# A state-space scan and its feed-forward block on one core: how the first two pairs of chunks load C and their products of a

## The chip, the cores and the metric

The kernel runs on one core of a Trainium2 chip. A core has five engines that run side by side: TensorE (PE: matrix products, its weight loads shown as PEld), VectorE (DVE), ScalarE (ACT), GpSimd (POOL) and SyncE (SP), which here does nothing but issue DMA transfers. ScalarE can issue transfers too. All transfers are moved by the same 16 DMA engines. The metric is the device time of one execution in microseconds; three runs of the kernel before took 359.32, 360.47 and 360.80 us, median 360.47.

## The reference

Two blocks, one after the other. First a selective state-space scan over 4 batches, 8 heads, 768 tokens, head dimension 32 and state size 16, in chunks; then a feed-forward block with a parametric ReLU on the 3072 tokens of 256 features that come out.

```python
# per batch and head; a in (0, 1], cum = running sum of log(a) in a chunk
L = np.exp(cum[..., :, None] - cum[..., None, :]) * causal      # decay from j to i
y_intra = einsum('ij,jd->id', (C @ B.T) * L, x)
y_inter = (C @ state) * exp(cum)
state = exp(sum(la)) * state + sum_j B_j x_j * exp(cum_end - cum_j)
# then, over all tokens
h = y @ w_in                                   # 256 x 2048
g = maximum(h, 0) + alpha * minimum(h, 0)
out = g @ w_out                                # 2048 x 256
```

All inputs are float32 but w_in and w_out, which arrive as float64 and have to be turned into float32 on the core.

## The kernel before

**Tiles.** The 3072 tokens are 24 chunks of 128 tokens. Two chunks make a pair (12 pairs), two pairs a group of 512 tokens (6 groups). The feed-forward block works on groups: hidden features 128 at a time (w_in, PReLU), then products with w_out. Group 0 uses plain products (`hidden`, `hidden_two`, `output`); groups 1 to 5 use a scheme of seven block products in the place of eight (`quad`, `product`), between which the scan stages of the next pairs are placed (`ssm`).

**Decays.** No logarithm is taken: the decay from j to i is a running product of a. Multiply-add scans on VectorE make it, with a (its first element of each chunk zero) as the factor and an identity as the addend. Pairs 0 and 1 are done by `first_two`, in quarter chunks of 64 tokens (`HQ`). There, TensorE spreads a from "(head, state) on partitions" to 64 partitions (`spread`, L852), VectorE scans the result (`scan`, L858), the gram of B and C is made by TensorE (`gram_of`, L868) and multiplied into it (`times`, L874). `added` (L882) makes the new states' increments, `states` (L897) chains them, `mask` (L903, GpSimd) spreads them by heads, `x_products` (L916) and `state_products` (L928) give y, which `copy_out` (L936) writes as xT, the input of the feed-forward block.

From pair 2 on the running products come from DRAM: `rows_products` (L438) scans all rows of a, writes them (`pf`, L441), and `load_products` (L167) reads them back, spread over partitions, as `ap` of a pair. Pair 2's state (L631) and its decays (L556, from `abc`, another spread copy) follow on VectorE.

**Layouts of B and C in pairs 0 and 1.** B is loaded with one token on each partition (`nat[:, 0, k]`, L203; 64-byte pieces) and turned by TensorE (`turned_b`, L842). C is loaded by `load_blocks` (L191) in 512-byte pieces, four blocks of 32 partitions, and turned by a 32 x 32 transpose on VectorE (`turned_c`, L828). C times a parity mask gives `cz` (L836, ScalarE). For pair 0, C is loaded by ScalarE's queue, all else by SP.

**Pair 0's and 1's running products** (`pf0`, `pf1`) come from a scan over their own a (`running`, L958), after `first_a` (L530 and L433) has made the scan's input.

**Weights.** Each of 16 pieces of 512 KB (`load_next`, L254) is made float32 by ScalarE (L270, L280 or L283), VectorE or GpSimd (L275), VectorE (sign bits, L293; L305), and at last GpSimd (L327). The pieces alternate between w_in and w_out from the second on.

**Fillers.** `keep_warm` (L335) issues products of constants whose result nobody reads.

**Order.** The schedule is written out by hand: each engine runs its instructions, and SP issues its transfers, in the order of the code. A transfer that waits holds back all that SP issues after it. SP's order at the start is: a, B, x of pair 0; a of pair 1; two w_in pieces; z (rows of a); C, B, x of pair 1; a w_in and a w_out piece; B, C, x of pair 2; five weight pieces; pf; abc; a weight piece; ap.

Of the kernel before, what the change touches and what calls it, by code (L numbers as in the profile page):

```python
# [22 lines left out]
def kernel(  # L23
# [47 lines left out]
    WARM = 512  # L71
# [97 lines left out]
    def load_pair(gp, decays=True):  # L169


        b, c = divmod(2 * gp, CPB)
        turned = gp > GC
        nat = ldx.tile([P, 3, 2, H * N], F32, name="nat")
        xt = ldx.tile([P, 2, HD], F32, name="xt")

        ap = ldx.tile([P, 2 * Q], F32, name="ap")
        if gp == 0:
            load_a(ap, b, c)
        elif gp > NB:  # L180
            load_products(gp, ap)
        if gp == 0:
            load_rows(0, nc.scalar)
        abc = []
        later = []

        def load_blocks(o, src, e, eng=nc.sync):


            first = src[b, e : e + 1, c * Q : (c + 2) * Q, :]  # L190
            eng.dma_start(out=o, in_=bass.AP(tensor=first.tensor, offset=first.offset,  # L191
                                             ap=[[2 * S * N, P // 32], [8 * N, 32], [1, 8 * N]]))

        for e in range(2 if gp < NB else 0):
            load_blocks(nat[:, 1, e], C, e, nc.sync if gp else nc.scalar)
        if gp == 0:
            nc.scalar.dma_start(out=al_n, in_=moe_alpha.rearrange("(k p) -> k p", p=P))
        if gp >= HALF:
            load_tokens(nat[:, 0], B[b], c * Q)
        for k in range(2 if gp < HALF else 0):  # L200
            ts = slice((c + k) * Q, (c + k + 1) * Q)
            for i, src in enumerate((B,) if turned or gp < NB else (B, C)):
                nc.sync.dma_start(out=nat[:, i, k].rearrange("p (h n) -> p h n", h=H),  # L203
                                  in_=src[b, :, ts, :].rearrange("h p n -> p h n"))

            def load_x(k=k, ts=ts):
                nc.sync.dma_start(out=xt[:, k].rearrange("p (h d) -> p h d", h=H),
                                  in_=x[b, :, ts, :].rearrange("h p d -> p h d"))

            if gp < NB:  # L210
                later.append(load_x)
            else:
                load_x()
        for load_x in later:
            load_x()
        if gp == 0:
            loads["a", 1] = prep.tile([P, 2 * Q], F32, name="a1")
            load_a(loads["a", 1], b, c + 2)
        for i, src in enumerate((B, C) if turned else ()):

            for e in range(2):
                load_blocks(nat[:, 1 + e, i], src, e)
        for k in range(2 if gp >= NB else 0):
            abc.append(lda.tile([P, H * Q], F32, name="abc"))
        loads["p", gp] = nat, abc, xt, ap
        if gp >= HALF:
            load_tokens(xt, x[b], c * Q)
        if decays:
            load_spread(gp, b, c)

# [106 lines left out]

    keep_warm(ps_h.tile([P, GT], F32, name="hp"), 1, WARM)
    keep_warm(ps_h.tile([P, GT], F32, name="hp"), 1)
# [4 lines left out]
    for v in range(2):  # L344
        vs = slice(HQ * v, HQ * (v + 1))
        nc.vector.tensor_copy(out=ident_q[vs].rearrange("p (c t) -> p c t", c=4),
                              in_=ident[vs, vs].unsqueeze(1).to_broadcast([HQ, 4, HQ]))
    bmask = const.tile([P, HD], F32, name="bmask")
# [17 lines left out]

    lent = [gp.tile([P, 4, Q], F32, name="gt", tag="gt") for i in range(4)]
# [3 lines left out]
    starts = [t.rearrange("p k t -> p (k t)") for t in (lent[0][:, :2], lent[3][:, 2:])]  # L371
    nc.gpsimd.memset(starts[0], 0.0)
# [109 lines left out]
    def rows_short(r):  # L482


        nc.vector.memset(r[:, ::HQ], 0.0)
        pr = lent[3][:RW, 1]
        nc.vector.tensor_tensor_scan(out=pr[:, ::-1], data0=r[:, 1:][:, ::-1],
                                     data1=ends_q[:RW, ::-1], initial=0.0, op0=ALU.mult,
                                     op1=ALU.add)
        return pr  # L490
# [319 lines left out]
    def first_two():  # L810
# [15 lines left out]
        def turned_c(nat):  # L826
            bc = work.tile([P, 4, Q], F32, name="bc")
            nc.vector.transpose(  # L828
                bc[:, 2:].rearrange("p k t -> p (k t)").rearrange("p (c b) -> p b c", b=8),
                nat[:, 1].rearrange("p e (b n) -> p b e n", n=N))  # L830
            return bc
# [7 lines left out]

        def turned_b(nat, tp, bc):  # L840
            for k in range(2):
                nc.tensor.transpose(tp[:, k * P : (k + 1) * P], nat[:, 0, k], ident)  # L842
            nc.scalar.copy(out=bc[:, :2].rearrange("p k t -> p (k t)"), in_=tp[:, : 2 * Q])
# [99 lines left out]
        def ss():  # L943
            return ps_s.tile([P, 512], F32, name="ss")
# [12 lines left out]
        def running(i, z, pf):  # L957
            nc.vector.tensor_tensor_scan(out=pf, data0=z.rearrange("p k t -> p (k t)"),  # L958
                                         data1=starts[i], initial=0.0, op0=ALU.mult,
                                         op1=ALU.add)  # L960

# [5 lines left out]
        clamp(nc.gpsimd, starts[0][:, ::HQ], ap0[:, ::HQ])  # L967
# [5 lines left out]
        load_pair(1)  # L973
        nat1, _, xt1, pf1 = loads["p", 1]
        scan(0, 0, sp[0])
        bc0 = turned_c(nat0)
        for r in range(1, 4):
            scan(0, r, sp[r])
        rows_turn("short", prq)
        tp = spare()  # L980
        turned_b(nat0, tp, bc0)
# [6 lines left out]
        hp = spare()  # L988
        keep_warm(hp, 1)
        gram_of(bc0, cz0, sp)  # L990
        dps = dps_in([hp, tp])
        added(dps, bn0, xt0)
        for r in (0, 1):
            times(0, r, sp[r])
        running(0, z0, pf0)
        nc.gpsimd.memset(starts[1], 0.0)
        z1 = first_a(loads["a", 1], nc.gpsimd, lent[1][:, 2:])
        clamp(nc.gpsimd, starts[1][:, ::HQ], loads["a", 1][:, ::HQ])
        cd0 = decayed_c(bc0, pf0)
        states(0, dps, pf0)  # L1000
        one_at_a_time(0, range(3))
        for r in (2, 3):
            times(0, r, sp[r])
        load_next(2)
# [9 lines left out]
        keep_warm(sp[0], 1)  # L1014
# [9 lines left out]
        bc1 = turned_c(nat1)  # L1024
# [5 lines left out]
        running(1, z1, pf1)  # L1030
        bn1 = pair_loads(1)
        convert_next(first=False)
        cz1 = spread_c(bc1)
        own = [ss(), ss()]
        turned_b(nat1, own[0], bc1)
        dps = dps_in(own)
        added(dps, bn1, xt1)
# [3 lines left out]
        states(1, dps, pf1, range(3))  # L1041
        gram_of(bc1, cz1, sp)
        one_at_a_time(1, range(3))
        for r in range(4):
            times(1, r, sp[r])
        states(1, dps, pf1, (3,))
        prelu_of[0]()
        convert_a(*pieces[2])
        sign(*pieces[2])

        def among(i, k):
            if (i, k) == (1, 0):
# [5 lines left out]
        prelu_of[2] = hidden_two(0, 2, 0, spare(), among)  # L1058
# [363 lines left out]
    sign(*pieces[3])  # L1422
# [141 lines left out]
```

## Time and profile before

| | |
|---|---|
| runs (us) | 359.32, 360.47, 360.80; median 360.47 |
| profiled execution | 360.79 us, span of its instructions 359.1 us |
| TensorE busy | 351.4 us (98%), 2979 products |
| VectorE, ScalarE, GpSimd busy | 239.5, 171.5, 204.6 us |
| DMA | 30.06 MB, of which the SP queue 29.25 MB, in 34.9% of the 16 engines' time |
| granted TensorE clock | 0.99 of full speed over the span |

All times in the profile are microseconds from the first instruction. Lines of the page give an engine's busy time; the chain of waits follows the last instruction back through what released each step; a timeline gives each instruction's start, length, source line, operands and, in brackets, how long the engine had been idle and what ended that. "x2" after a matrix product counts machine instructions: a float32 product is two. L numbers are lines of the kernel before.

### The profile page before, as it was taken

What the parts mean: (1) busy time and instruction counts of PE and PEld (TensorE: products, weight loads), DVE (VectorE), ACT (ScalarE), POOL (GpSimd) and SP (SyncE); (2) the same over time, 40 slices, a digit from 0 to 9 for tenths busy, and PEclk for the clock granted to TensorE, in tenths of its full rate; (3) what the DMA queues carried; (4) which work ended last, traced back from release to release, by engine and by line L of the source; (5) the groups of instructions that cost most, each with busy time, mean ns of one, the idle gap of its engine ahead of it and who ended that gap; (6) DMA issues with size and microseconds to landing.
All of it is one profiled execution on the core that took longest, in us unless ns stands there. A gap on an engine that the chain in (4) does not pass through costs nothing.

```text
span 359.1 us, 7762 instructions
## 1 busy us (share of the span) xinstructions
PE 351.4 (98%) x2979; PEld 286.7 (80%) x2979; DVE 239.5 (67%) x483; ACT 171.5 (48%) x389; POOL 204.6 (57%) x229
## 2 busy tenths in 40 slices
PE   6999999999999999999999999999999999999996
PEld 3676656668888888888888888888888888888885
DVE  6798795998937856866656856657856634643363
ACT  3358746535354445445345445445445444443431
POOL 6667548579847947526546536537536545434510
PEclk9699999999999999999999999999999999999999
DMA  6899889505436502402522421521101001001102
GB/s 130 184 190 355 238 215 240 135 2 120 127 88 145 108 3 62 101 15 57 91 62 53 92 64 48 97 64 43 32 2 29 2 2 29 2 1 29 33 0 58
DMA packets 101701, 30.06 MB, mean 84 GB/s; under 512 B 75728, under 2 KB 97568, under 8 KB 101664
## 3 DMA queue, kind: packets, MB, share of 16 engines
q1 hardware_dynamic: 100984, 29.25, 34.9%
q8 instruction: 23, 0.38, 0.4%
q10 hardware_dynamic: 680, 0.32, 0.3%
q14 instruction: 14, 0.11, 0.1%
HBM read 26.19 MB, written 3.37 MB: 82 GB/s over the span
## 4 chain that ended last, share of the span: by engine, by line
PE 89%; DMA 4%; DVE 4%; ACTq 0%; issue 0%; POOL 0%; ACT 0%; DVEq 0%
PE bank L1199 33%; PE hp L1224 28%; PE bank L1125 6%; PE ss L1224 6%; PE hp L1078 3%; DMA pf<-rpf 2%; PE ss L776 1%; DVE dec L556 1%; PE ss L720 1%; DMA ap<-pf 1%; DMA nat<-in_C_dram 1%; PE bank L335 1%; PE bank L1192 1%; PE ss L794 1%; PE ss L768 1%; PE bank L868 1%
## 5 line engine op out<-in xcount | busy, mean ns | idle before, releaser
L1281 POOL TENSOR_TENSOR gt<-gt 128x512 f32<-128x512 f32 x58 | 74.2, 1279 | 21.1 <-DVE gt L1209 16.2
L1199 PE MATMUL bank<-gt,w_out 128*128 128x256 f32 x320 | 83.6, 382 | 0.0
L1199 PEld LDWEIGHTS bank<-gt,w_out 128*128 128x128 f32 x320 | 60.3, 190 | 9.1 <-issue 1.0
L1209 DVE SCALAR_TENSOR_TENSOR gt<-hp,s_mul,gt 128x256 f32<-128x256 f32 x96 | 42.0, 479 | 29.0 <-ACT gt L1207 26.8
L1271 POOL TENSOR_TENSOR gt<-gt 128x512 f32<-128x512 f32 x20 | 25.4, 1271 | 62.9 <-DVE gt L1209 57.0
L1207 ACT ACTIVATE gt<-hp,s_alpha 128x256 f32<-128x256 f32 x96 | 40.3, 471 | 34.6 <-PE hp L1224 31.4
L1199 PE MATMUL bank<-gt,ws 128*128 128x256 f32 x224 | 55.9, 379 | 0.0
L1199 PEld LDWEIGHTS bank<-gt,ws 128*128 128x128 f32 x224 | 42.4, 190 | 5.5
L1224 PE MATMUL hp<-xs,w_in 128*128 128x256 f32 x160 | 41.9, 385 | 0.0
L1224 PE MATMUL hp<-xs,ws 128*128 128x256 f32 x160 | 41.2, 380 | 0.0
L1250 DVE TENSOR_TENSOR hp<-hp,u 128x512 f32<-128x512 f32 x20 | 14.0, 700 | 35.2 <-ACT u L1248 35.2
L1224 PEld LDWEIGHTS hp<-xs,ws 128*128 128x128 f32 x160 | 30.4, 190 | 4.3 <-POOL xs L1166 0.2
L1224 PEld LDWEIGHTS hp<-xs,w_in 128*128 128x128 f32 x160 | 29.8, 190 | 4.4
L1125 PE MATMUL bank<-w_out,gt 128*128 128x256 f32 x128 | 31.2, 386 | 0.9 <-POOL w_out L327 0.9
L1125 PEld LDWEIGHTS bank<-w_out,gt 128*128 128x128 f32 x128 | 23.6, 190 | 7.9 <-issue 3.1
L1224 PE MATMUL ss<-xT,w_in 128*128 128x256 f32 x96 | 24.6, 379 | 0.0
L634 POOL TENSOR_TENSOR sm<-state,bmask 128x256 f32<-128x256 f32 (+1 forms) x10 | 6.2, 619 | 29.8 <-DVE state L631 29.8
L1078 PE MATMUL hp<-xT,w_in 128*128 128x512 f32 x48 | 22.8, 597 | 0.0
L550 DVE TENSOR_TENSOR_SCAN dec<-abc,bank 128x192 f32<-128x192 f32 x48 | 22.7, 523 | 0.0
L1239 ACT COPY m<-hp 128x512 f32<-128x512 f32 x8 | 4.7, 586 | 35.7 <-PE hp L1224 35.7
L1248 ACT COPY u<-hp 128x512 f32<-128x512 f32 x20 | 11.7, 585 | 19.4 <-PE hp L1224 19.4
L1209 DVE SCALAR_TENSOR_TENSOR gt<-c,s_mul,gt 128x256 f32<-128x256 f32 x40 | 20.6, 556 | 0.0
(231 smaller groups left out, 614.2 us busy)
## 6 DMA issues: line engine op xcount, KB each, us to landing
abc<-z SPq DMA_DIRECT2D x24, 192.0 KB
raw<-in_moe_w_in_dram SPq DMA_DIRECT2D x8, 512.0 KB
raw<-in_moe_w_out_dram SPq DMA_DIRECT2D x8, 512.0 KB
abc<-z SPq DMA_DIRECT2D x8, 512.0 KB
out_dram<-o_sb SPq DMA_DIRECT2D x32, 64.0 KB
nat<-in_B_dram SPq DMA_DIRECT2D x26, 64.0 KB
xt<-in_x_dram SPq DMA_DIRECT2D x12, 128.0 KB
xt<-in_x_dram SPq DMA_DIRECT2D x24, 64.0 KB
```

Of the source, the lines that this page charges most:

```text
L550: nc.vector.tensor_tensor_scan(out=dv[:, o : o + SQ], data0=abc[k][:, s : s + SQ], data1=ident_p[0][:, :SQ], initial=0.0, op0=ALU.mult, op ...
L634: nc.gpsimd.tensor_tensor(out=sm[:, :nk].rearrange("p k (g m) -> p k g m", g=2), in0=new[:, :nk].unsqueeze(2).to_broadcast([P, nk, 2, 2 * D]),
L1078: nc.tensor.matmul(hp, w_in[:, k, f * P : (f + 1) * P], xts[g][:, k], start=(k == 0), stop=(k == KC - 1))
L1125: nc.tensor.matmul(pos[0][t // 2][:, t % 2], gt[:, t * Q : (t + 1) * Q], w_out[:, f], start=(f == 0 and t % 2 == 0), stop=(f == NF - 1), s ...
L1199: nc.tensor.matmul(ms[g][i][:, h], w, blocks[g, z][n][:, p], start=(q == 0 and h == 0), stop=(q == NQ - 1), skip_group_check=True)
L1207: nc.scalar.mul(o[:, p], h[:, p], s_alpha[:, fs[p]])
L1209: nc.vector.scalar_tensor_tensor(out=o[:, p], in0=h[:, p], scalar=s_mul[:, fs[p]], in1=o[:, p], op0=ALU.mult, op1=ALU.max)
L1224: nc.tensor.matmul(to[:, p], w(2 * z + p), b, start=start and p == 0, stop=True, skip_group_check=True)
L1248: nc.scalar.copy(out=u2, in_=A)
L1250: nc.vector.tensor_tensor(out=Y, in0=Y, in1=u2, op=ALU.add)
L1271: nc.gpsimd.tensor_tensor(out=tc_, in0=g22, in1=g12, op=ALU.subtract)
L1281: eng.tensor_tensor(out=o, in0=x0, in1=x1, op=ALU.subtract)
```

## The change

Only the part up to `first_two`'s end is changed.

- C of pairs 0 and 1 is loaded like B, one token per partition; pair 0's still by ScalarE's queue. `turned` turns both with TensorE, and ScalarE copies C, then B.
- Pair 1's running products are no longer scanned from its own a: `rows_short` also scans all rows of a in quarter chunks, writes them to DRAM (`short`), and `load_second` reads pair 1's part back. Pair 0's scan (`running`) stays, earlier in VectorE's order.
- `first_a` of pair 1 moves from GpSimd to VectorE.
- Fillers: two of 512 columns at the start in the place of 512 and 256; one of 512 in the place of 256 before pair 0's gram; the one of 256 before pair 0's state products goes.
- Pair 1's `added` and `states`, then its gram, `times` and the PReLU of the first hidden products, are issued between the products of the second `hidden_two` (by `among`), not ahead of them.
- After `first_two`, piece 3's `convert_b` (sign bits and L305) comes at once, not only its sign bits.

```diff
-    WARM = 512
+    WARM = 2
...
-        def load_blocks(o, src, e, eng=nc.sync):
-            first = src[b, e : e + 1, c * Q : (c + 2) * Q, :]
-            eng.dma_start(out=o, in_=bass.AP(tensor=first.tensor, offset=first.offset,
-                                             ap=[[2 * S * N, P // 32], [8 * N, 32], [1, 8 * N]]))
-        for e in range(2 if gp < NB else 0):
-            load_blocks(nat[:, 1, e], C, e, nc.sync if gp else nc.scalar)
...
-            for i, src in enumerate((B,) if turned or gp < NB else (B, C)):
-                nc.sync.dma_start(out=nat[:, i, k].rearrange("p (h n) -> p h n", h=H),
-                                  in_=src[b, :, ts, :].rearrange("h p n -> p h n"))
+            for i, src in enumerate((B,) if turned else (B, C)):
+                eng = nc.scalar if gp == 0 and i else nc.sync
+                eng.dma_start(out=nat[:, i, k].rearrange("p (h n) -> p h n", h=H),
+                              in_=src[b, :, ts, :].rearrange("h p n -> p h n"))
...
+    def load_second():
+        rows = scratch["short", 0].rearrange("(b h c) t -> b h (c t)", b=2, h=H)
+        nc.sync.dma_start(out=loads["p", 1][3], in_=rows[0, :, 2 * Q : 4 * Q].unsqueeze(1)
+                          .to_broadcast([H, N, 2 * Q]))
...
-    keep_warm(ps_h.tile([P, GT], F32, name="hp"), 1, WARM)
-    keep_warm(ps_h.tile([P, GT], F32, name="hp"), 1)
+    keep_warm(ps_h.tile([P, GT], F32, name="hp"), WARM, GT)
...
+        rpf = lent[3][:RW, 3]
+        nc.vector.tensor_tensor_scan(out=rpf, data0=r[:, :Q], data1=starts_r[:RW], initial=0.0,
+                                     op0=ALU.mult, op1=ALU.add)
+        scratch["short", 0] = dr.tile([RW, Q], F32, name="short0")
+        nc.sync.dma_start(out=scratch["short", 0], in_=rpf)
...
-        def turned_c(nat):
+        def turned(nat, banks):
             bc = work.tile([P, 4, Q], F32, name="bc")
-            nc.vector.transpose(
-                bc[:, 2:].rearrange("p k t -> p (k t)").rearrange("p (c b) -> p b c", b=8),
-                nat[:, 1].rearrange("p e (b n) -> p b e n", n=N))
+            for i, tp in enumerate(banks):
+                for k in range(2):
+                    nc.tensor.transpose(tp[:, k * P : (k + 1) * P], nat[:, i, k], ident)
+            for i in (1, 0):
+                nc.scalar.copy(out=bc[:, 2 * i : 2 * i + 2].rearrange("p k t -> p (k t)"),
+                               in_=banks[i][:, : 2 * Q])
             return bc
...
         load_pair(1)
+        load_second()
         nat1, _, xt1, pf1 = loads["p", 1]
-        scan(0, 0, sp[0])
-        bc0 = turned_c(nat0)
-        for r in range(1, 4):
+        for r in range(4):
             scan(0, r, sp[r])
         rows_turn("short", prq)
-        tp = spare()
-        turned_b(nat0, tp, bc0)
+        tp, hp = spare(), spare()
+        bc0 = turned(nat0, (tp, hp))
...
-        hp = spare()
-        keep_warm(hp, 1)
+        keep_warm(hp, 1, GT)
         gram_of(bc0, cz0, sp)
         dps = dps_in([hp, tp])
         added(dps, bn0, xt0)
+        nc.vector.tensor_tensor_scan(out=pf0, data0=z0.rearrange("p k t -> p (k t)"),
+                                     data1=starts_a, initial=0.0, op0=ALU.mult, op1=ALU.add)
+        cd0 = decayed_c(bc0, pf0)
         for r in (0, 1):
             times(0, r, sp[r])
-        running(0, z0, pf0)
-        nc.gpsimd.memset(starts[1], 0.0)
-        z1 = first_a(loads["a", 1], nc.gpsimd, lent[1][:, 2:])
-        clamp(nc.gpsimd, starts[1][:, ::HQ], loads["a", 1][:, ::HQ])
-        cd0 = decayed_c(bc0, pf0)
...
+        z1 = first_a(loads["a", 1], nc.vector, lent[1][:, 2:])
...
-        keep_warm(sp[0], 1)
         state_products(y, 0, cd0)
...
-        bc1 = turned_c(nat1)
...
-        running(1, z1, pf1)
         bn1 = pair_loads(1)
         convert_next(first=False)
-        cz1 = spread_c(bc1)
         own = [ss(), ss()]
-        turned_b(nat1, own[0], bc1)
+        second = spare()
+        bc1 = turned(nat1, (own[0], second))
+        cz1 = spread_c(bc1)
         dps = dps_in(own)
-        added(dps, bn1, xt1)
         mask(0, slice(3, 4))
...
         def among(i, k):
+            if (i, k) == (0, 0):
+                added(dps, bn1, xt1)
+                states(1, dps, pf1, range(3))
+                one_at_a_time(1, range(3))
+            if (i, k) == (0, 1):
+                gram_of(bc1, cz1, sp)
+                for r in range(4):
+                    times(1, r, sp[r])
+                states(1, dps, pf1, (3,))
+                prelu_of[0]()
+                convert_a(*pieces[2])
+                sign(*pieces[2])
             if (i, k) == (1, 0):
...
-        prelu_of[2] = hidden_two(0, 2, 0, spare(), among)
+        prelu_of[2] = hidden_two(0, 2, 0, second, among)
...
     convert_a(*pieces[3])
-    sign(*pieces[3])
+    convert_b(*pieces[3])
     hidden_two(0, 0, 2 * Q, spare())()
```

## The prediction

> **What bounds the kernel now.** I read the page first (shares, then the 40 slices), then the chain of waits for the first 85 us, then the timelines of VectorE, TensorE and the SP queue at the places the chain names, and last a table of the DMA share by stretch.
>
> From the page, the slices:
>
> ```profile
> PE   6999999999999999999999999999999999999996
> PEclk9699999999999999999999999999999999999999
> DMA  6899889505436502402522421521101001001102
> ```
>
> TensorE is full from the second slice to the end, so the time is TensorE's work plus what it idles early; nothing after 50 us is touched by the change. The DMA engines are full in slices 2 to 7 (9 to 63 us) only.
>
> From the chain of waits, 20 to 50 us (start, length, what):
>
> ```profile
> 26.10 1.35 DVE rpf L438
> 27.47 7.29 DMA pf<-rpf
> 34.77 4.17 DMA ap<-pf
> 39.04 0.28 DVE state L631
> 39.32 2.33 DVE dec L556 x4
> ...
> 43.43 2.33 DVE dec L556 x4
> ...
> 47.61 1.27 POOL w_out L327
> 48.92 1.13 PE bank L1125 x4
> ```
>
> In this stretch TensorE does not set the end. The running products of all rows go to DRAM (pf) and come back for pair 2 (ap), 11.5 us for 176 KB, and VectorE then works without a gap to the weights that TensorE waits for. The two idle times that close the chain, from the timelines of VectorE and TensorE:
>
> ```profile
> 39.04 0.28 DVE L631 SCALAR_TENSOR_TENSOR state<-gt,ap,ss 128x64 f32<-128x64 f32 x1 [1.58 <-DMA ap<-pf]
> 48.92 1.35 PE L1125 MATMUL bank<-w_out,gt 128*128 128x256 f32 x5 [0.43 <-POOL w_out L327]
> ```
>
> So TensorE has 0.43 us of slack against this chain at 48.9 us: TensorE work saved earlier is lost again here, and a later ap is paid in full.
>
> Why the pf write takes 7.29 us is in the SP timeline and the DMA share:
>
> ```profile
> 9.16 3.90 SPq L203 DMA_DIRECT2D nat<-in_B_dram  x2
> ...
> 17.42 3.65 SPq L207 DMA_DIRECT2D xt<-in_x_dram  x1
> ...
> 26.11 0.45 SPq L254 DMA_DIRECT2D raw<-in_moe_w_in_dram  x1
> 27.47 0.33 SPq L441 DMA_DIRECT2D pf<-rpf  x1
> ```
>
> ```profile
> 11.00:15.00 4.00, 4.00 (x57) 1.51 (x39) 3.54 (x10) 1.16 (x3) 3.03 (x7) 0.50 0.53 87
> 24.00:34.00 10.00, 9.52 (x69) 7.34 (x70) 8.95 (x18) 8.55 (x22) 5.70 (x6) 1.00 1.03 315
> ```
>
> (the last three columns are the granted clock, the DMA share and GB/s). Five weight pieces of 512 KB stand ahead of pf in the same queue, at share 1.03; the queue has run without a pause since 0.8 us, SP being held 3.4 us at 9.7 and 3.65 us at 17.4. The pf write lands when the queue has drained, not when VectorE is ready. What the change does to the end is what it does to this queue. And from 11 to 15 us, where C and B of pair 1 are moved, the queue is held up though the share is only 0.53: some engines hold back the others.
>
> **What the Trainium skill says.** "DMA: Bandwidth & Descriptors", section "Why a DMA increments its semaphore by 16 and not by 1": a DMA from SP or ACT is split over the largest number of engines, up to 16, that divides the slowest dimension of both sides, on the lowest-numbered ones; the issuer adds the rest of the count at once. The trace agrees: the semaphore of pair 0's first C load (slowest dimension 4 in the block pattern) counts one early update at 2.49 us and four late ones up to 4.87; the load of a for pair 0 (slowest dimension 8 heads) one and eight; B loads count sixteen. Same page, "Issuing engines are not separate DMA queues": loads issued by ACT share the 16 engines with SP's; B's first load ends at 3.8 to 4.0 us on twelve engines and at 5.1 to 5.2 on the four that also carry ACT's C. "TensorE: Matmul & The Clock Gate", "What's actually happening": the clock is decided in free-running windows of 3.41 us; the trace shows half clock from 8.5 to 15.3 us, two such windows.
>
> **The change part by part.** Packet times are means of the trace's packet records: 64 B 10.7 ns, 512 B 27.8, 1 KB 48.3, 128 B 12.6.
>
> *C loads.* Removed: four block loads, each 128 packets of 512 B on four engines, 32 x 27.8 = 0.89 us on each. Added: four token loads of 1,024 packets of 64 B on sixteen engines, 64 x 10.7 = 0.69 us on each. On the first four engines that is 4 x (0.69 - 0.89) = -0.8 us; on the other twelve +2.7 us, which they had free (share 0.53).
>
> *Pair 1's running products.* Added on SP: the write of 96 rows (6 x 27.8 = 0.17 us per engine) ahead of z, and their read back, heads outermost, so eight engines, 16 x 48.3 = 0.77 us. The read waits for the write; the four B and C and two x loads stand between, some 6 us, so no wait.
>
> *Sum on the queue.* First four engines: -0.8 + 0.17 + 0.77 = +0.1 us. The next four end at the same time (they gain the 3.56 us of block load they lacked), the rest earlier. Upper end: pair 2's six small loads took 5.7 us (19.73 to 25.44, first tenths of the packets) for 4 x 0.69 + 2 x 0.81 = 4.4 us of engine time, a factor 1.3; put on the four new loads, 4 x 0.69 x 0.3 = +0.8. Between +0.1 and +0.9 I take +0.4. Lower end: the last block load of pair 1 took 1.2 us from first tenth to last against 0.55 for the B load after it; if blocks really cost 1.1 and tokens 0.6, 4 x -0.5 + 0.94 = -1.1.
>
> *VectorE.* Removed: two transposes (0.64 each) and pair 1's scan (0.70). Added: a scan over 96 rows (0.42, as L487) before TensorE's spread is done (it waited 0.79 there), and first_a of pair 1 (0.35, as L433 and L530 of pair 0) ahead of the first weights. All of it ends before L631, whose 1.58 us of idle covers 0.4 us; uncovered it would be 0.4.
>
> *ScalarE.* Two C copies, 0.37 each (L843). For pair 0: C copy, B copy, then cz. Before, from C's landing, 0.64 transpose + 0.91 cz; now 0.33 of TensorE, 0.37 + 0.3, 0.91: 0.4 later, against C landing 0.4 earlier (four token loads behind ap, 3.1 + 4 x 0.69 + 0.4 of receipt = 6.25 against 6.62). Zero.
>
> *GpSimd.* 1.8 us (L996, L530, L433 of pair 1) leaves the way of cd and the masks.
>
> *TensorE.* First filler +256 columns: L335 took 2.90 us for 768, so up to +0.5 after the wait of 0.42 for z is used; the scans behind it end earlier anyway without the transpose among them. Filler before the gram +256 at full clock, 0.4, inside the 0.64 wait for cz. The filler before the state products goes: 1.15 us. Pair 1: four transposes instead of two (+0.2), hidden products put between, which fill the 0.51 idle at 19.7. convert_b of piece 3 before the first rest: removes the 0.48 idle at 31.7. Together about -1.5 us for TensorE by 48 us, which the 0.43 slack then turns into waiting.
>
> *Sum:* span 359.1 + 0.4 = 359.5; the profiled execution is 360.79 for that span, 1.7 more, so 361.2, and it is 0.3 above the median of 360.47: **360.9**.
>
> **Rivals.** (1) *Total DMA work, not the fullest engines, sets the queue*: then all added busy time counts, 4 x (1,024 x 10.7 - 128 x 27.8)/16 = 1.85, plus 0.17, plus 128 x 48.3/16 = 0.39, together +2.4 us at pf: 362.9. For it: share 1.03 from 24 us on. Against: 0.53 from 11 to 15 us, and completion waits for the slowest engine. It decides, slower by over 0.5%, when a token load costs the queue 0.35 us more than my 0.1-to-0.9 account gives it, that is over 1.1 us each. (2) *The clock*: without the 256-column filler the window 11.9 to 15.3 is not busy enough and full clock comes one or two windows later; 3.4 to 6.8 us at half clock cost TensorE 1.7 to 3.4 us. Against it stand the 1.5 gained and 0.43 slack: 0 to +1.5 beyond, and with the queue's own shift up to 362.4. For it: the windows are unaligned to the kernel. Against: filler and products still fill that window. (3) *Blocks were the brake*: queue shift -1.1, or more if SP is freed earlier at 9.7 to 13; TensorE has about 1.9 to give. 359.4, at best 358.6. Against: the two new transfers are certain, the saving is not. (4) *The change doesn't move the clock or the queue at all*: same as the forecast.
>
> **How the numbers follow.** What a measurement of this kernel can tell from no change is about 0.5%, 1.8 us. Forecast 0.52, with its own range 359.7 to 362.1; rival 1 0.25; rival 2 0.12 (half of it beyond 0.5%); rival 3 0.11 (half of it beyond). To this I add some weight to slower for late data of pair 1, which now queues six loads of 64 B and 128 B and a read back before its products. Faster 0.10, same 0.53, slower 0.37. Range 359.0 to 364.0: the lower end holds the milder half of rival 3, the upper rival 1 with a microsecond for late data.
>
> **What would show it.** Right: VectorE's wait before the pair 2 state grows from 1.58 us by more than TensorE gains, ap lands at 38.9 + 0.4, TensorE's wait at L1125 grows from 0.43 to some 2 us; DMA share from 11 to 15 us rises towards 0.9; TensorE's first hidden products start near 16.3 instead of 17.1. Rival 1: ap lands after 41. Rival 2: half clock past 15.3. Rival 3: ap lands before 38 and TensorE no longer waits at 48.9. It would be wrong if B, C or x of pair 1 landed after 19 us, or if another chain than pf and ap bound before 50 us.

## The result and the profile after

The changed kernel takes 361.92 us (median of 20 executions, 360.76 to 364.28), the kernel before 360.96 us (20 executions taken beside them). The ratio is 1.0036, with a 95% interval of 1.0018 to 1.0054: about a microsecond longer, and within the 0.5% that the prediction calls no difference, though the interval reaches just past it. The profiled execution took 361.22 us, with a span of 359.5 us. One execution of the kernel before, beside a later experiment, took 601.86 us at a granted clock of 0.565 and is left out of all that follows.

The page of the kernel after, the same three rows in 40 slices of 9 us:

```profile
PE   8889999999999999999999999999999999999996
PEclk9988999999999999999999999999999999999999
DMA  8999999205436502502522521531201001001102
```

Before, the granted clock dipped in the second slice (0.6). Now it is at 0.9 there and dips in the third and fourth. The records of the clock place it: before, half clock from 8.48 to 15.30 us; after, full from 6.47 us, and half from 23.54 to 30.36. Both are two windows of 3.41 us.

The chain of waits of the kernel after, for the same stretch (start, length, what):

```profile
15.72 0.70 DVE wr L305
...
16.55 1.27 POOL w_in L327
...
17.87 0.70 PE hp L1092 x2
...
21.99 1.05 issue
23.05 0.41 PE bank L922 x20
...
25.26 4.56 PE hp L1092 x10
29.83 2.06 PE bank L1092 x8
...
49.65 0.45 PE bank L1124 x2
```

No DMA stands in it after 6.28 us: in this execution TensorE itself sets the end. The answering line of VectorE's timeline:

```profile
39.26 0.28 DVE L637 SCALAR_TENSOR_TENSOR state<-gt,ap,ss 128x64 f32<-128x64 f32 x1 [0.16 <-DMA ap<-pf]
```

and those of TensorE's, the first a filler of 512 columns:

```profile
10.32 1.13 PE L335 MATMUL bank<-const-float32-1.0 128*128 128x512 f32 x2
...
13.98 2.25 PE L1092 MATMUL hp<-xT,w_in 128*128 128x256 f32 x8
...
17.87 0.70 PE L1092 MATMUL hp<-xT,w_in 128*128 128x256 f32 x2 [1.20 <-POOL w_in L327]
...
23.05 0.41 PE L922 MATMUL bank<-dec,xt 64*32 64x64 f32 x20 [1.05 <-issue]
...
25.19 4.63 PE L1092 MATMUL hp<-xT,w_in 128*128 128x256 f32 x10
```

In the kernel before, the two groups of hidden products were these:

```profile
17.09 1.89 PE L1093 MATMUL hp<-xT,w_in 128*128 128x256 f32 x8
...
25.27 2.43 PE L1093 MATMUL hp<-xT,w_in 128*128 128x256 f32 x10
```

Pair 2's state starts at 39.26 us instead of 39.04, and VectorE waits 0.16 us for ap instead of 1.58. The transfer is not earlier; VectorE is later, since its own input comes from TensorE: between 29 and 33 us it twice stands idle for over a microsecond (1.11 and 1.18) until ScalarE has passed on TensorE's hidden products. The first hidden products start at 13.98 us instead of 17.09, so TensorE is 3.1 us ahead. It then idles 1.20 and 1.05 us, and the ten hidden products that took 2.43 us before (at 25.27 us) take 4.63 us at half clock. The product group that began at 48.92 us before begins at 49.65 us in the chain.

The table by stretch (columns: busy time of TensorE, weight loads, VectorE, ScalarE, GpSimd; granted clock, DMA share, GB/s):

```profile
11.00:15.00 4.00, 4.00 (x84) 2.52 (x83) 3.81 (x11) 3.19 (x8) 2.17 (x4) 1.00 0.74 89
21.00:24.00 3.00, 1.93 (x72) 1.43 (x64) 2.84 (x9) 0.00 (x0) 0.58 (x2) 0.92 0.77 90
24.00:34.00 10.00, 10.00 (x40) 7.65 (x41) 5.84 (x11) 6.20 (x17) 4.14 (x5) 0.68 1.00 317
```

The share from 11 to 15 us is 0.74 instead of 0.53. From 24 to 34 us TensorE has no idle time left and a clock of 0.68.

### The profile page after: what moved, and what is told of

It is laid out like the page before. It is cut to its first block, busy times and chain, and to the rows that moved or that the text cites. A ratio compares the mean times of both kernels' runs of the same rounds, so it can differ in the third digit from the quotient of the medians.

```text
span 359.5 us, 7769 instructions
## 1 busy us (share of the span) xinstructions
PE 352.6 (98%) x2981; PEld 286.4 (80%) x2981; DVE 239.6 (67%) x483; ACT 172.3 (48%) x391; POOL 202.2 (56%) x227
## 4 chain that ended last, share of the span: by engine, by line
PE 96%; DMA 1%; DVE 1%; issue 0%; POOL 0%; SPq 0%; ACT 0%; POOLq 0%
PE bank L1198 33%; PE hp L1223 28%; PE bank L1124 8%; PE hp L1077 6%; PE ss L1223 6%; PE hp L1092 2%; PE ss L782 1%; PE ss L726 1%; DMA nat<-in_B_dram 1%; PE bank L1191 1%; PE ss L800 1%; PE ss L774 1%; PE ss L737 1%; PE bank L1092 1%; PE ss L613 1%; PE ss L934 0%
## 5 line engine op out<-in xcount | busy, mean ns | idle before, releaser
L1280 POOL TENSOR_TENSOR gt<-gt 128x512 f32<-128x512 f32 x58 | 74.2, 1278 | 21.1 <-DVE gt L1208 16.3
L1208 DVE SCALAR_TENSOR_TENSOR gt<-c,s_mul,gt 128x256 f32<-128x256 f32 x40 | 20.6, 555 | 0.0
```

The costliest lines, as they stand in the source:

```text
L1208: nc.vector.scalar_tensor_tensor(out=o[:, p], in0=h[:, p], scalar=s_mul[:, fs[p]], in1=o[:, p], op0=ALU.mult, op1=ALU.max)
L1280: eng.tensor_tensor(out=o, in0=x0, in1=x1, op=ALU.subtract)
```

## Reading the times by the granted clock

Half-clock windows do not fall in the same place, or in the same number, in every execution, so the executions are grouped below by mean granted clock. One window of 3.41 us at half clock takes 3.41 x 0.5 / 360 = 0.005 off the mean. A mean of 0.998 or more is therefore no window, 0.993 to 0.997 one, 0.988 to 0.992 two, and less three or more. The mean counts from the first record of the clock, so half clock ahead of that record is not in it; of the kernels with the fillers of before, "none" may hold executions that were at half clock until 13 us (two profiles below were). Mean times in us, with the number of executions; the kernel before is taken from the executions beside the experiments:

| kernel | no window recorded | one | two | three or more |
|---|---|---|---|---|
| before | 361.09 (83) | 363.11 (16) | 361.57 (60) | 364.07 (15) |
| after | 361.35 (4) | 362.14 (8) | 362.40 (6) | 364.12 (2) |

Without a recorded window the difference is +0.26 us, which four executions with a standard deviation of 0.43 can't tell from nothing; the four sets of the kernel before differ among themselves by as much (360.80 to 361.29 us without a window). Sixteen of the 20 executions of the changed kernel have one or more windows, and the means of these groups lie 0.8 us and more above that of the four.

## The experiments

The theory to test had four parts: the chain over pf and ap sets the end, the change leaves the DMA queue ahead of it about where it was, TensorE's early gain is lost in waiting for that chain, and the clock takes the rest. The rivals were total DMA work, blocks as the brake, and the clock as the main cause.

### Pair 1's products from rows, alone

The kernel before with this one edit (the scan on VectorE, the write and the read back on SP), and pair 1's own scan gone:

```diff
+        nc.vector.tensor_tensor_scan(out=rpf, data0=r[:, :Q], data1=starts_r[:RW], ...)
+        nc.sync.dma_start(out=scratch["short", 0], in_=rpf)
...
         load_pair(1)
+        load_second()
...
-        running(1, z1, pf1)
```

> The kernel before with one part of the change alone: pair 1's running products from DRAM (the extra write, the read back, pair 1's own scan gone). Queue theory: +0.17 +0.77 us on the fullest DMA engines, nothing else, so +0.9 us against before, ap for pair 2 about 0.9 later than 38.9 us. Rival (total DMA work sets the queue): 0.17 + 0.39 = +0.6. Rival (clock): no change beyond what the clock of the run gives.

Measured: 362.98 us (11 executions), ratio 1.0041 (1.0008 to 1.0074), so 1.35 us over the kernel before beside it (361.63). Three executions without a recorded window had a mean of 361.55, or +0.46 to the table above, with a standard deviation of 0.94. The chain of waits of its profile:

```profile
35.36 5.19 DMA ap<-pf
...
40.64 0.28 DVE state L644
40.92 2.33 DVE dec L569 x4
```

The state is at 40.64 us where it was at 39.04, and the same chain carries it. The edit costs something, and the interval of the ratio (+0.3 to +2.7 us) holds the expected +0.9 and the rival's +0.6 alike. Without a window its size is half of the expected, but three executions don't settle that.

### C one token per partition, alone

```diff
-        for e in range(2 if gp < NB else 0):
-            load_blocks(nat[:, 1, e], C, e, nc.sync if gp else nc.scalar)
...
-            for i, src in enumerate((B,) if turned or gp < NB else (B, C)):
+            for i, src in enumerate((B,) if turned else (B, C)):
+                eng = nc.scalar if gp == 0 and i else nc.sync
...
-        bc0 = turned_c(nat0)
+        bc0 = turned(nat0, (tp, hp))
```

> The kernel before with the other part alone: C of the first two pairs by tokens, turned by TensorE, order and fillers as before. Queue theory (blocks hold four engines): the queue is 0.8 us shorter, and TensorE has 0.43 us of slack to give, so -0.4 us, between -0.8 and 0. Rival (total DMA work): +1.85 us. Rival (clock): -1 to +2, following the granted clock.

Measured: 361.17 us (14), ratio 1.0000 (0.9980 to 1.0021); without a window 361.15 (10), against 361.09 of the kernel before. By the rival of total DMA work the token loads alone were worth +1.85 us, 0.5%, which the interval (-0.7 to +0.8 us) excludes: that rival falls. The expected gain of -0.4 us isn't seen, but lies inside the interval and is not excluded. Without windows the two edits sum to +0.46 + 0.06 = +0.5 us, against +0.26 for the whole change, all three within the noise. The profile of this run fell on a long execution (364.09 us), and shows how late ap can be:

```profile
41.75 0.28 DVE L629 SCALAR_TENSOR_TENSOR state<-gt,ap,ss 128x64 f32<-128x64 f32 x1 [5.17 <-DMA ap<-pf]
46.19 0.48 PE L729 MATMUL hp<-cz,bc 32*128 32x256 f32 x1 [3.24 <-DVE gt L1074]
```

### More fillers where the changed kernel's TensorE idles

The changed kernel with three fillers of 256 columns at 16.7 us, and one of 512 ahead of pair 1's state products:

```diff
+        keep_warm(sp[3][:, 2 * Q :], 3)
         cz1 = spread_c(bc1)
...
                 x_products(y, xt1, 1)
+                keep_warm(sp[3], 1, GT)
                 state_products(y, 1, cd1)
```

> The changed kernel with fillers where its TensorE idled 1.2 us at 16.7 us (3 of 256 columns) and one of 512 before pair 1's state products. If the changed kernel's later end comes from half-clock windows after 20 us: full clock from 7 us on in nearly every run, the time set by ap alone, 361.3, that is 0.6 below the changed kernel, and little spread. If the clock is not its cause: 361.9 or more, since 2.1 us of fillers are added.

Measured: 361.80 us (22), ratio 1.0008 (0.9987 to 1.0029). Without a window in 14 of 22 executions (mean 361.89), where the changed kernel had 4 of 20. So the fillers do move the clock. But the time stays where it was: the 361.3 us that was expected if the windows make the changed kernel longer did not come, and 361.89 without a window is what was expected if they don't. Since the fillers cost TensorE time of their own (a later experiment puts that at 1.5 us once the chain is gone), this run doesn't decide whether the windows make the +0.96 us of the medians. Its profile has no half clock before the last microseconds, and this is the line of VectorE's timeline:

```profile
41.94 0.28 DVE L637 SCALAR_TENSOR_TENSOR state<-gt,ap,ss 128x64 f32<-128x64 f32 x1 [4.49 <-DMA ap<-pf]
```

and this one is of TensorE's:

```profile
46.38 0.48 PE L737 MATMUL hp<-cz,bc 32*128 32x256 f32 x1 [2.48 <-DVE gt L1083]
```

With the clock full, VectorE waits 4.49 us for ap and TensorE 2.48 us behind it: the early gain turns into waiting, as the prediction had it. That execution was a long one (363.68 us), and its ap is 2.7 us later than in the profile of the changed kernel, with the same transfers in the same order. A single profile does not place ap to better than that: in the profiles of the other runs with pf behind the weights, the state starts at 40.10 to 41.75 us, later than in those of both the kernel before and the changed kernel.

### pf and ap ahead of the weights, in the changed kernel

The rows' running products are written as soon as the rows are there (their scan moves with them), and read back ahead of the weight pieces in SP's order:

```diff
     def rows_products():
-        d0 = held.pop(0)
+        d0 = held[0]
...
+        rows_products()
         rows_out(0)
...
         load_pair(2, False)
+        load_products(NB, loads["p", NB][3])
         load_next(2)
...
         held["pr"] = rows_scan(0)
-        rows_products()
...
-    load_products(NB, loads["p", NB][3])
```

> The changed kernel with the write of all rows' running products and their read back for pair 2 ahead of the weight pieces in SP's queue, so that the chain over pf and ap is gone. If that chain holds the changed kernel when the clock is full: 1 to 3 us faster than the changed kernel in runs at full clock (358.5 to 360.5), no gain in runs with two half-clock windows (361.5 to 363). If the chain does not matter: 361.9.

Measured: 359.52 us (22), ratio to the kernel before 0.9950 (0.9928 to 0.9973), so below both kernels. By windows: none 358.18 (8), one 359.31 (8), two 361.69 (6). In VectorE's timeline the state waits for nothing:

```profile
37.30 0.27 DVE L637 SCALAR_TENSOR_TENSOR state<-gt,ap,ss 128x64 f32<-128x64 f32 x1
```

and after 10 us TensorE's keeps only the two early idle times:

```profile
17.82 0.70 PE L1093 MATMUL hp<-xT,w_in 128*128 128x256 f32 x2 [1.20 <-POOL w_in L327]
...
23.00 0.41 PE L922 MATMUL bank<-dec,xt 64*32 64x64 f32 x20 [1.06 <-issue]
```

Without a window the edit takes 361.35 - 358.18 = 3.2 us off: that is what the chain over pf and ap cost the changed kernel there. The edit takes VectorE's scan (1.35 us in the kernel before) out of the chain as well as the transfers; the two were not tried apart. With two windows it takes off only 0.7, and two windows now cost 3.5 us, about the 6.83 / 2 = 3.4 that TensorE loses in them. The chain and the windows hide each other.

### pf and ap ahead of the weights, in the kernel before

The same edit, in the kernel before.

> The kernel before, with the write of pf and the read of ap put ahead of the weight pieces in SP's order (the edit that took 3.2 us from the changed kernel at full clock). In its profile TensorE had 0.43 us of slack against the chain over pf and ap while it had run two half-clock windows (8.5 to 15.3 us). Theory (the chain holds the kernel before as well, TensorE is next): in executions with those two windows -0.4 us (about 361.0), in executions at full clock from the start up to 3.4 us less (about 358), median 359.5 to 361. Rival (the chain became the bound only by the change): no difference, 361.3 at every clock. In the profile the wait of VectorE for ap at pair 2's state is gone.

Measured: 359.09 us (22), ratio 0.9948 (0.9930 to 0.9966). By windows: none 359.41 (11), two 359.02 (8), three 360.61 (3). In its profile the state starts at 36.45 us without a wait, with half clock from 7.30 to 14.12 us. So the chain held the kernel before as well, and the rival of no difference falls; but the sizes were wrong twice. In executions with two windows the edit gives some 2.5 us (361.57 to 359.02), not 0.4. Those without a recorded window take 359.41, no less than those with two, where some 358 was expected; with the fillers of before, they may have been at half clock early as well. Its chain of waits shows what is left:

```profile
29.89 1.29 POOL w_out L327
31.23 1.99 PE bank L1126 x8
...
46.99 1.99 PE bank L1126 x8
```

The place of w_out in the kernel before is this:

```profile
32.16 1.99 PE L1125 MATMUL bank<-w_out,gt 128*128 128x256 f32 x8 [0.48 <-POOL w_out L327]
```

After w_out at 31.23 us it is TensorE alone. From there to the product group that waited at 48.92 us before, the kernel before took 48.92 - 32.16 = 16.76 us and this one 46.99 - 31.23 = 15.76: the chain cost 1.0 us in this stretch, of which the last wait showed 0.43. The other 0.93 us between the two profiles stand already at the ten hidden products (24.34 against 25.27 us), ahead of the scan that heads the chain; in the profiles of the two parts of the change alone, the products behind w_out also start at 31.23 and 31.27 us, so the kernel before's own profile seems to have been late there by chance.

With pf and ap early in both kernels, the ratio to the kernel before is 0.9950 with the change and 0.9948 without it. So it is not only the chain that hides TensorE's early gain: uncovered, the change is worth nothing in the median either. It is shorter without a recorded window (358.18 against 359.41) and longer with two (361.69 against 359.02).

### The order of pair 1's work, put back

The changed kernel with masks, states, gram and terms of pair 1 ahead of the second group of hidden products, as before:

```diff
-        def among(i, k):
-            if (i, k) == (0, 0):
-                added(dps, bn1, xt1)
-                states(1, dps, pf1, range(3))
-                one_at_a_time(1, range(3))
-            if (i, k) == (0, 1):
-                gram_of(bc1, cz1, sp)
...
+        added(dps, bn1, xt1)
+        states(1, dps, pf1, range(3))
+        one_at_a_time(1, range(3))
+        gram_of(bc1, cz1, sp)
```

> The changed kernel with pair 1's masks, states, gram and terms put back ahead of the first hidden products, as the kernel before has them; tokens, rows and fillers as changed. Theory (the chain over pf and ap sets the end, TensorE's order ahead of it is worth nothing at full clock): 361.3 at full clock, as the changed kernel (361.35), median 361.3 to 362.2. Rival (the order is what gained TensorE its 3 us by 17 us and is worth it at the end): 363 or more. In the profile the first hidden products move from 14.0 us back to 16 or later.

Measured: 362.24 us (22), ratio 1.0033 (1.0016 to 1.0050), against 1.0036 of the changed kernel; without a window 361.09 (2). No worth of the order is seen at the end while the chain stands, as the theory says. One detail failed: the first hidden products did not move back to 16 us, since they stand ahead of the moved block in either order; it is the second group that the edit moves.

The same order with pf and ap early:

> The same order put back, with pf and ap early so that the chain doesn't cover TensorE. Theory (uncovered, TensorE's waiting for pair 1's data in the order of before shows): 1 to 3 us over the changed kernel with pf and ap early at the same clock (358.2 at full clock), so 359.2 to 361.2 at full clock. Rival (the order is worth nothing even uncovered; TensorE waits for the same data either way): 358.2 at full clock, median within 0.5 of 359.5.

Measured: 359.58 us (22), ratio 0.9940 (0.9914 to 0.9966); without a window 359.11 (6), one 359.33 (9), two 361.28 (6). Without a window the changed order is worth 359.11 - 358.18 = 0.9 us uncovered, at the lower end of the theory's 1 to 3; with one or two windows (359.33 against 359.31, 361.28 against 361.69) and in the median (359.58 against 359.52) nothing is seen. So the reordering gains TensorE at most a little, and only at full clock.

### The fillers of before, put back

```diff
-    keep_warm(ps_h.tile([P, GT], F32, name="hp"), WARM, GT)
+    keep_warm(ps_h.tile([P, GT], F32, name="hp"), 1, 512)
+    keep_warm(ps_h.tile([P, GT], F32, name="hp"), 1)
...
-        keep_warm(hp, 1, GT)
+        keep_warm(hp, 1)
...
+        keep_warm(sp[0], 1)
         state_products(y, 0, cd0)
```

> The changed kernel with the fillers of before (512 and 256 columns at the start instead of two of 512, 256 instead of 512 ahead of pair 0's gram, 256 ahead of pair 0's state products). Theory (the fillers only move the half-clock windows; the chain over pf and ap sets the end): 361.3 at full clock as the changed kernel (361.35), and the windows come back early (about 8.5 us, as before) where they cost nothing at the end, so fewer of the executions over 362: median 361.2 to 361.6. Rival (the windows are set by TensorE's own idle at 18 and 22 us, whatever the fillers): windows at 23 us as changed, median 361.9 or more.

Measured: 362.38 us (19), ratio 1.0043 (1.0016 to 1.0070); no recorded window in 6 of 19 executions (361.62), three or more in 5 (364.77). TensorE's timeline of its profile:

```profile
11.46 1.95 PE L335 MATMUL bank<-const-float32-1.0 128*128 128x512 f32 x2
...
16.33 1.89 PE L1094 MATMUL hp<-xT,w_in 128*128 128x256 f32 x8
...
44.89 0.48 PE L738 MATMUL hp<-cz,bc 32*128 32x256 f32 x1 [2.44 <-DVE gt L1083]
```

The filler of 512 columns at 11.46 us took 1.95 us, where it took 1.13 at 10.32 us in the changed kernel: half clock until 13.15 us, the first record. The first hidden products start at 16.33 us, not 13.98. So of the 3.1 us by which TensorE was ahead there, the fillers made some 2.35, most of it through the clock (the filler that came back ahead of the state products takes 0.70). These are single profiles: in that of the run with more fillers, at full clock, the same products start at 14.55 us. In all nine profiles of kernels with the changed fillers the clock is full from 6.9 us or earlier to 19 us or later; in none of the five with those of before is it. The half clock early came back, as the theory had it, but the shorter median did not: 13 of the 19 executions have recorded windows as well (where, is known of the profiled one alone), and the median is the rival's. The one profile again shows the early loss as no loss, since TensorE waits 2.44 us at 44.89 behind the chain (VectorE 4.28 us for ap).

### Both: pf and ap early, with fillers

The changed kernel with pf and ap early, and all four extra fillers:

> The changed kernel with pf and ap early and with the extra fillers at 16.7 us and ahead of pair 1's state products. Theory (TensorE now sets the end, and the half-clock windows are paid in full): most executions at full clock, 358.2 plus up to 1 us for the fillers, 358.5 to 359.2, so 0.3 to 1 us below the same edit without the fillers (359.52). Rival (the fillers cost what they save): 359.5 or more, with most executions at full clock nevertheless.

Measured: 360.03 us (22), ratio 0.9973 (0.9956 to 0.9991); without a window 359.68 (14), where the kernel without extra fillers had 358.18. The rival holds: no window in most executions, and a price of 1.5 us for it. With only the three fillers of 256:

> The changed kernel with pf and ap early and only the three fillers of 256 columns at 16.7 us, which lie ahead of TensorE's wait of 1.20 us for w_in; the one of 512 ahead of the state products is left out. Theory (the 512 filler was paid in full, some 0.9 us, and the three are hidden in the wait): 358.2 to 358.8 at full clock, most executions at full clock, median 358.5 to 359.0. Rival (any filler on TensorE is paid once the chain is gone): full-clock executions at 359.2 or more, and a median not below 359.5.

Measured: 359.07 us (7), ratio 0.9939 (0.9915 to 0.9963); without a window 358.98 (6). Between the two accounts: the fillers cost 0.8 us without windows and gain 0.45 in the median, from seven executions. The chain of waits of its profile had a new head:

```profile
27.78 10.05 DMA abc<-z
37.85 2.42 DVE dec L562 x4
...
46.23 1.27 POOL w_out L327
47.55 1.99 PE bank L1126 x8
```

Once ap is early, the next transfer in the same queue binds: pair 2's decay rows.

### The decay rows ahead of three weight pieces

```diff
         load_products(NB, loads["p", NB][3])
         load_next(2)
+        load_spread(2, *divmod(4, CPB))
...
-        load_spread(2, *divmod(4, CPB))
```

> The changed kernel with pf and ap early and the three fillers of 256, and the reads of pair 2's decay rows (abc from z, two of 512 KB) put ahead of three of the weight pieces in SP's order. In the profile of the kernel without this last edit the chain of waits ran over these reads (issued 27.78, landed after 10.05 us) and VectorE's scans to a TensorE wait of 0.43 us at 47.55. Theory (they are the next bound): the scans start some 2 us earlier and TensorE's wait is gone, 358.98 less 0.4 at full clock, so 358.4 to 358.7, median 358.5 to 358.9. Rival (the three weight pieces, 1 MB later, are then late themselves): TensorE waits for w_in or w_out before 40 us, 359.5 or more.

Measured: 358.70 us (15), ratio 0.9920 (0.9895 to 0.9946); without a window 358.43 (10), one 359.75 (5). The lowest median of all the kernels run here, 0.8% below the kernel before, and both numbers lie where the theory had them. The interval overlaps that of the run before it (0.9915 to 0.9963), so the step from one to the other is not clear of the noise. In its profile VectorE's scans no longer wait for abc, and TensorE has no idle time over 0.3 us after 24.4 us.

### The idle time put down to issue

The changed kernel with eight fillers of 64 columns at 16.7 us, one execution:

```diff
+        keep_warm(sp[3][:, 2 * Q :], 8, 64)
         cz1 = spread_c(bc1)
```

> The changed kernel with eight fillers of 64 columns at 16.7 us. TensorE's idle of 1.05 us, put down to issue, came ahead of the last 20 of pair 1's products of dec and x; with three more fillers ahead of it, ahead of the last 26. Theory (TensorE stops at one place of its instruction stream, not for any data): two products earlier for each filler, so ahead of the last 36. Rival (it waits for data or for a time): ahead of the last 20 still, or no such idle.

Measured: 361.80 us, and no such idle time in its profile, so the theory as written fell, and this outcome is one of the two that the rival named. What it leaves is under the last heading.

## Why the prediction was right, point by point

The forecast of 360.9 us within 359.0 to 364.0, "same" the likeliest, was right: the median is 361.92 and the ratio within 0.5%. The difference to the kernel before was forecast at +0.4 us and measured at +0.26 us without windows, which is within the noise, and +0.96 in the medians, with an interval of +0.65 to +1.95 us that leaves +0.4 out. The verdict holds; that the number comes within 1.0 us is in part luck. TensorE's early gain (3.1 us at the first hidden products, where 0.8 was expected) and its loss to later half clock (3.4 us in the profiled execution) were both larger than put, and they nearly cancel.

*The chain over pf and ap sets the end before 50 us.* Shown, in both kernels: pf and ap early shorten the changed kernel by 3.2 us without windows, and the kernel before 2.3 in the median beside it (361.38 to 359.09).

*"TensorE has 0.43 us of slack against this chain."* This step was wrong in its size. Without the chain the kernel before ends about 2 us earlier (1.2 to 2.5). Two things were missed. TensorE's last wait is what remains after the chain has already delayed it elsewhere: the stretch from 31 us to that wait is 1.0 us longer with the chain than without. And that wait is no measure of slack: it reads 0.43 or 0.44 us in five profiles with pf behind the weights, whether TensorE had waited for pair 2's gram before (0.94, 2.44, 2.48 us) or not. The profile was also one with an early ap: pair 2's state starts at 39.04 us in it, and at 40.10 to 41.94 in six of the seven others with pf behind the weights. The forecast did not suffer, since the step was only used to say that TensorE's gain would be lost.

*The sum on the DMA queue, +0.1 to +0.9, taken as +0.4.* Neither shown nor refuted. The rows were put at 0.17 + 0.77 = 0.94 and measured +0.46 without windows, +1.35 in the medians; the C loads at -0.8 on the fullest engines, and measured +0.06 without windows. The noise is as large as these differences. In the profiles the state moved 0.22 us, but one profile doesn't place it so well. The DMA share from 11 to 15 us rose to 0.74, part of the way to 0.9. That loading C by tokens changes the time by more than 0.8 us either way is excluded; a small gain or loss is not. The Trainium skill's section "Why a DMA increments its semaphore by 16 and not by 1" in "DMA: Bandwidth & Descriptors", on how a DMA is split, fits the trace of the changed kernel too: the read back of pair 1's products, heads outermost, shows one early update of its semaphore at 15.72 us and eight late ones up to 17.88. What it does not give is whether the fullest engines bind here.

*VectorE, ScalarE and GpSimd at zero.* Nothing in the runs speaks against it. All of C, B and x of pair 1 had landed by 17.1 us, before the 19 us from which the prediction would have been wrong.

*TensorE, "about -1.5 us by 48 us", turned into waiting.* The kind was right, the size was not: the first hidden products start at 13.98 us, where the prediction said 16.3. (16.33, in the run with the fillers of before, is another kernel at another clock; that it agrees is luck.) What failed is the pricing of the fillers by their columns (the first at up to +0.5 us, the one ahead of the gram at 0.4, hidden): in fact the clock is at full from 6.47 us on with them, which is most of the difference. The sign that was named, a wait of some 2 us on TensorE, stands in profiles at full clock (2.48 us with more fillers, 2.44 with the fillers of before), though at pair 2's gram and not at the product group of 48.9 us. In the profiled execution of the changed kernel it is absent: there the two idle times and the later half clock took the gain first.

*Rival 2, the clock.* Right that it moves, wrong in place and sign of the first step, and underrated at 0.12. The prediction feared the window from 11.9 to 15.3 us for want of the filler of 256; that stretch is now at full clock. The windows come later: in the six of nine profiles with the changed fillers that have any before 50 us, the first starts between 19.26 and 25.94 us. Executions with windows are longer on average, but that windows make the whole +0.96 us of the medians is not shown. The Trainium skill's "TensorE: Matmul & The Clock Gate", section "Why this matters for your kernels", warns of idle gaps over about 3 us between bursts; here half clock came at 23.54 us with no gap of TensorE over 1.20 us between 4 us and it, so keeping below the page's gap was not enough. What tips a window stays open. The fillers at 16.7 us and ahead of the state products raised the share of executions without one from 4 of 20 to 14 of 22, which speaks for TensorE's idling at 17.9 and 23.0 us. Against it, a profile with three fillers has a gap of 1.55 us ahead of 18.03 and no window, and the one with eight fillers of 64 columns has two windows from 19.26 us without the second gap.

*Rival 1, total DMA work*: refuted by the tokens alone (ratio 1.0000). *Rival 3, blocks as the brake*: refuted by the same run, since the 4 x 0.5 = 2 us that it gives the loads lie outside the interval. *Rival 4*, that nothing moves: the time is near it, but the clock did move, by both early fillers and late windows.

## What to carry to other kernels

A wait at the end of a chain is not the chain's price: here it read 0.43 us and the chain cost about 2. Move the transfer that heads the chain and time that, before working on an engine that the chain covers. Where a clock that steps in windows is in play, look at the times by granted clock before naming a cause: under the chain two windows cost about 1.05 us, and once the chain was gone 3.5. When transfers share one queue in order, the small one that a chain hangs on belongs ahead of the large ones that nobody waits for yet; here that, with its scan moved forward too, was worth 3.2 us without windows and 2.4 in the medians, where the whole change gained nothing.

## What the runs showed of the hardware

- The same program on the same data had none, one, two or three half-clock windows, and with pf and ap early its times lie in steps by that number: 358.18, 359.31, 361.69 us.
- Some 500 more filler columns, 256 at the start and 256 ahead of the first gram, had the clock at full from 7 to 19 us in nine profiles of nine; with the shorter fillers it was so in none of five: three have records of 6.83 us at half between 7.30 and 15.36 us, and in the other two, whose first records are at 13.15 and 13.82 us, a filler of 512 columns ahead of these took 1.95 and 2.07 us in the place of 1.13. Which of the two does it was not tried.
- TensorE stopped for 1.05 us at a place where no releaser is seen, ahead of the last 20 of pair 1's products of dec and x. The place was the same, to the product, in four profiles with different orders and queues (stops of 1.05, 1.06, 2.32 and 2.05 us), and ahead of the last 26 in three with three more fillers of 256 (0.65, 1.03 and 1.47 us). That points to a place in the instruction stream. In these a 16 KB transfer of the queue that the profile's page calls instruction runs from 20.6 to 22.2 us on, and TensorE goes on about 1.3 to 1.5 us after its end; with eight more fillers, and with the fillers of before, that transfer came at 15.8 and 18.3 us and there was no stop. One more profile with three fillers has the transfer at 20.74 us and no stop over 0.3 us, and so has the kernel before, with the transfer at 21.63. A late fetch of instructions would explain this, but nothing here shows whose instructions they were, and it stays open.
